# w2's low halves on VectorE, four w2 buffers, two steps moved to GpSimd, and a new planned order

## The chip, the core and the metric

The kernel runs on one core of a Trainium2 chip. The metric is the device time of one launch in microseconds, the median of several runs. The core has four compute engines that run side by side, each through its own queue in the order that the program fixes: TensorE (PE in the profile; matmuls and transposes, results in PSUM), VectorE (DVE), ScalarE (ACT) and GpSimd (POOL). A fifth queue, SyncE (SP), issues DMAs.

## The reference

Attention with a top-32 mask in float32, then two feed-forward blocks with float64 weights, each block's result rounded to float32; 2 x 576 tokens, 8 heads of 64.

```
scores = q @ k.T / 8                    # per head, 576 x 576
kth = 32nd largest of each row
scores = where(scores >= kth, scores, -1e9)
attn = exp(scores - max); attn = attn / (attn.sum(-1) + 1e-9)
x = concat_heads(attn @ v)              # 1152 x 512
h = x @ w_in                            # 2048 wide
x = (max(h, 0) + alpha * min(h, 0)) @ w_out
out = ((x @ w_a) * (x @ w_b)) @ w_out2  # 1536 wide
```

## The kernel before

**Work and groups.** The query rows are cut into six groups (M1, counted 0 to 5): two of 128 tokens from the first batch, three of 256 tokens, one of 128. Every group's attention consists of tiles of 128 query rows of one head, 72 in all. A tile's scores go through TensorE (`front`), then VectorE finds the 32 largest by four rounds of MAX8 and three of MATCH_REPLACE8 (`middle`, lines 1094 to 1103) and multiplies mask and exponentials with a running sum (line 1110, tiles e and sm). ScalarE adds 1e-9 to that sum (line 1111), VectorE takes the reciprocal (line 1117), and GpSimd scales e with it (line 1118). `back` transposes (on TensorE for batch 0, by a transposing DMA on SP for batch 1), and `av` multiplies with v, one pair of heads at a time, into xT.

**The two feed-forward blocks.** Each group runs `moe1` and `moe2` in the order of ORDER and STAGES. `moe1`'s `l1` makes h (tiles h, from wi), the leaky relu follows, and `l2` projects with wo into y; `moe2`'s `l3` makes hab (from wa and wb) and `l4` projects with w2 into o. The first groups run in float32 ("native") weights; from the third group on, and in the first layer of the second group, a product is made of three half-precision passes ("split"): high times high, high times low, low times high.

**The relu of a native second layer.** GTM gives the way for groups 0, 1, 2. For 'd' (lines 1306 to 1312) ScalarE writes both relus, the negative one back into PSUM, and VectorE blends them in one instruction. For 'p' (lines 1309, 1317, 1318) the negative one goes to SBUF, and GpSimd multiplies it by minus alpha and adds the other. 'm' alternates by block.

**Weights.** Each 128 x 512 block of a weight comes as float64 and is converted (`to_f32`) by ScalarE, VectorE and GpSimd together; w2's 12 float32 blocks are then parked in device memory (w2_st). After `scales` (the tot matmul at line 764 and its copy at 766) `pair` turns blocks into a high and a low half: ScalarE scales into the tile wsc (tag tmp, one buffer) and rounds it to the high half, GpSimd subtracts for the low half. For w2 (lines 893 to 902) a block is loaded from w2_st into a w2s tile, the halves are made in a second w2s tile, and that is stored to w2_pr, from which `moe2` loads (line 1386). The w2s tiles are W2B = 3 buffers, handed out in the order of the program.

**Order.** `tile_topk_attention_moe` emits three tracks (attention and conversion, pairs, feed-forward). `keep_planned_order` then replays all instructions in a model of the chip (`planned_order`: durations from NS, a due time of each instruction from its place plus RANK, buffers handed out in turn) and fixes for every engine the order that comes out of it.

Of the kernel before, what the change touches and what calls it, by code (L numbers as in the profile page):

```python
# [11 lines left out]
F32 = mybir.dt.float32  # L12
# [29 lines left out]
W2B = 3  # L42
# [15 lines left out]
PAIRS = ("wi", "wo", "wa", "wb", "w2")  # L58
# [7 lines left out]
GTM = 'mdd'  # L66
# [26 lines left out]
    "ACT Activation Copy S4x1024h<-S4x1024f": (1056, 947, None),  # L93
    "ACT Activation Copy S4x128f<-P4x128f": (277, 157, None),
    "ACT Activation Copy S4x128f<-P4x128f,S4x1f": (367, 265, None),
    "ACT Activation Copy S4x128h<-P4x128f": (277, 173, None),
    "ACT Activation Copy S4x128h<-P4x128f,S4x1f": (367, 250, 2465),
    "ACT Activation Copy S4x128h<-S4x128f": (309, 258, None),
    "ACT Activation Copy S4x1f<-S4x1f": (203, 93, 2095),
    "ACT Activation Copy S4x256f<-P4x256f,S4x1f": (469, 357, 2863),  # L100
    "ACT Activation Copy S4x256h<-P4x256f": (383, 281, None),
    "ACT Activation Copy S4x256h<-P4x256f,S4x1f": (473, 356, None),
    "ACT Activation Copy S4x256h<-S4x256f": (416, 307, 2428),
    "ACT Activation Copy S4x256r<-S4x256f": (417, 306, None),
    "ACT Activation Copy S4x512f<-P4x512f": (597, 477, None),
    "ACT Activation Copy S4x512f<-S4x512f,S4x1f": (721, 613, None),
    "ACT Activation Copy S4x512h<-P4x512f,S4x1f": (687, 570, None),
    "ACT Activation Copy S4x512h<-S4x512f": (619, 520, None),
    "ACT Activation Copy S4x513s<-S4x513u": (791, 639, None),
    "ACT Activation Copy S4x576f<-P4x576f": (647, 530, 2039),  # L110
    "ACT Activation Copy S4x576h<-S4x576f": (683, 589, 2124),
    "ACT Activation Copy S4x576r<-S4x576f": (682, 574, None),
    "ACT Activation Copy S4x640f<-S4x640f,S4x1f": (829, 721, None),
    "ACT Activation Copy S4x640h<-S4x640f": (730, 627, None),
    "ACT Activation Copy S4x64h<-P4x64f": (218, 104, None),
    "ACT Activation Copy S4x64h<-P4x64f,S4x1f": (305, 196, None),
    "ACT Activation Copy S4x64r<-S4x64f": (244, 146, None),
    "ACT Activation Exp P4x576f<-S4x576f,S4x1f": (745, 666, None),
    "ACT Activation Relu P4x128f<-P4x128f": (284, 195, None),
    "ACT Activation Relu P4x128f<-P4x128f,S4x1f": (367, 249, 2425),  # L120
    "ACT Activation Relu S4x128f<-P4x128f": (272, 150, None),
    "ACT Activation Relu S4x128f<-P4x128f,S4x1f": (382, 249, 2465),
    "ACT Activation Sign S4x513b<-S4x513f": (777, 626, None),
    "ACT Activation Square S4x512f/<-P4x512f": (680, 570, None),
    "ACT Activation Square S4x640b/<-S4x640f": (824, 719, None),
    "ACT DMACopy  D2x512f<-S2x512f": (542, 580, 2660),
    "ACT DMACopy  D4x512f<-S4x512f": (338, 394, 2017),
    "DVE MatchReplace  S4x576f<-S4x8f,S4x576f": (811, 733, None),
# [1529 lines left out]
```

## Time and profile before

| | |
|---|---|
| runs (three) | 677.06, 678.73, 679.77 us; median 678.73 |
| profiled execution | 680.37 us, of which the span of its instructions 678.6 |
| granted TensorE clock, mean | 0.956 |
| busy: TensorE | 610.2 us (90%) |
| busy: VectorE | 552.0 us (81%) |
| busy: ScalarE | 482.6 us (71%) |
| busy: GpSimd | 435.8 us (64%) |
| DMA | 94.84 MB, 140 GB/s over the span |

The shares are means over phases with different limits. In the table of windows a window's first figure is its length; a busy time near it means that the engine is full there. In an order of time, the bracket at the end of a row gives the idle time before the instruction and what ended it. A group's "idle before" is the idle time of its engine just ahead of it. TensorE's clock has two levels, and the granted clock is a window's mean in shares of the higher.

### The profile page before, as it was taken

Reading aid. Unit: us, or ns where it says so; the run is one execution under the profiler, and the core shown is the slowest. Engines: PE = TensorE matmul, PEld = TensorE weight load, DVE = VectorE, ACT = ScalarE, POOL = GpSimd, SP = SyncE. Lnnn points to the kernel's source line nnn. Section 1 sums busy time; section 2 is a strip of 40 time slices with the busy share of each in tenths; the row PEclk is TensorE's granted clock in tenths of the full one; section 3 lists DMA queues with packets and bytes.
Section 4 is the critical chain, followed back from the end, with each engine's and each line's share of the span. In section 5 each row is a group of like instructions: output and inputs, shape, how many; then the busy total and the mean of one; then the engine's idle time right before and its main releaser. Section 6 shows DMA issues by size and latency. Waiting matters only on the chain.

```text
span 678.6 us, 14869 instructions
## 1 busy us (share of the span) xinstructions
PE 610.2 (90%) x5094; PEld 448.4 (66%) x5094; DVE 552.0 (81%) x1340; ACT 482.6 (71%) x1051; POOL 435.8 (64%) x648
## 2 busy tenths in 40 slices
PE   2466689999999999599979799999999999999997
PEld 1355477787766877467648477665877776777775
DVE  4999999869999999989999899999999997320021
ACT  5799999997899988799888455565655564642232
POOL 5787689976766877888988555554666556222221
PEclk9976689999999999699999899999999999999999
DMA  6997899984421132223576854522345332002243
GB/s 182 331 321 247 269 366 337 355 297 137 118 89 50 45 105 64 82 78 100 149 182 160 177 128 97 123 44 51 86 104 117 86 81 42 12 2 63 63 141 109
DMA packets 98491, 94.84 MB, mean 140 GB/s; under 512 B 50416, under 2 KB 72688, under 8 KB 98416
## 3 DMA queue, kind: packets, MB, share of 16 engines
q1 hardware_dynamic: 97104, 91.54, 47.7%
q10 hardware_dynamic: 1312, 2.36, 1.0%
q8 instruction: 40, 0.66, 0.4%
q14 instruction: 35, 0.29, 0.1%
HBM read 74.60 MB, written 8.65 MB: 123 GB/s over the span
## 4 chain that ended last, share of the span: by engine, by line
PE 42%; DVE 4%; DMA 4%; ACT 2%; issue 1%; POOL 0%; POOLq 0%; SPq 0%; ACTq 0%; DVEq 0%
PE hab L1258 13%; PE h L1258 9%; PE o L1270 8%; PE y L1270 7%; DMA w2s<-w_st 2%; PE ps L1083 2%; PE o L1170 2%; DVE wk L1101 1%; DVE m L1103 1%; DMA pt<-e 1%; DVE e L1110 1%; DMA kr<-in_kT_dram 1%; DVE yb L1344 0%; ACT w2s L900 0%; ACT wsc L899 0%
## 5 line engine op out<-in xcount | busy, mean ns | idle before, releaser
L1103 DVE MAX8 m<-wk 128x8 f32<-128x576 f32 x216 | 162.9, 754 | 2.3
L1249 POOL TENSOR_TENSOR gp<-gt,gp 128x256 f16<-128x256 f32 (+1 forms) x112 | 68.1, 612 | 79.9 <-ACT gp L1248 79.4
L1101 DVE MATCH_REPLACE8 wk<-m,wk 128x576 f32<-128x576 f32 x144 | 107.0, 743 | 0.0
L1258 PE MATMUL h<-xT,wi_sb 128*128 128x256 f16 (+1 forms) x960 | 99.2, 251 | 0.9 <-DVE gt L1299 0.9
L1258 PEld LDWEIGHTS <-wi_sb 128*128 128x128 f16 x960 | 78.4, 98 | 23.4 <-issue 8.5
L1270 PEld LDWEIGHTS <-gp 128*128 128x128 f16 x588 | 54.7, 98 | 55.1 <-issue 4.7
L1270 PE MATMUL y<-wo_sb,gp 128*128 128x512 f16 x336 | 81.4, 379 | 0.9 <-ACT gp L1248 0.9
L1118 POOL TENSOR_SCALAR e<-e,sm 128x576 f32<-128x576 f32 x72 | 54.0, 749 | 35.6 <-DVE sm L1117 33.2
L1248 ACT ACTIVATE gp<-gt 128x256 f16<-128x256 f32 (+1 forms) x112 | 43.0, 388 | 39.8 <-PE y L1270 13.6
L1258 PE MATMUL hab<-xT,wa_sb 128*128 128x256 f16 (+1 forms) x648 | 67.0, 249 | 3.9 <-ACT xT L1349 3.7
L1083 PE MATMUL ps<-ks,qh 128*128 128x288 f32 x160 | 47.0, 377 | 23.1 <-DVE e L1110 14.0
L1270 PE MATMUL o<-w2s,gp 128*128 128x512 f16 x252 | 64.8, 388 | 1.8 <-DMA w2s<-w_pr 1.6
L1258 PE MATMUL hab<-xT,wb_sb 128*128 128x256 f16 (+1 forms) x648 | 64.2, 249 | 0.0
L1258 PEld LDWEIGHTS <-wa_sb 128*128 128x128 f16 x648 | 52.1, 98 | 16.5 <-issue 4.1
L1094 DVE MAX8 m<-s 128x8 f32<-128x576 f32 x72 | 53.9, 749 | 10.2 <-ACT s L1086 10.0
L1110 DVE SCALAR_TENSOR_TENSOR e<-s,m,ep 128x576 f32<-128x576 f32 x72 | 58.3, 810 | 4.7 <-PE t L1143 1.3
L1431 DVE SCALAR_TENSOR_TENSOR gt<-hab,wb_inv,r 128x256 f32<-128x256 f32 (+1 forms) x36 | 15.6, 433 | 55.2 <-ACT r L1425 55.1
L1258 PEld LDWEIGHTS <-wb_sb 128*128 128x128 f16 x648 | 52.3, 98 | 4.1
L1107 ACT ACTIVATE ep<-s,nb 128x576 f32<-128x576 f32 x72 | 53.8, 747 | 1.5 <-ACT s L1086 0.4
L842 ACT ACTIVATE rlo<-raw 128x513 int16<-128x513 uint32 x68 | 52.4, 788 | 2.3 <-DMA raw<-in_wo_dram 1.8
L1101 DVE MATCH_REPLACE8 wk<-m,s 128x576 f32<-128x576 f32 x72 | 53.5, 743 | 0.0
L1086 ACT ACTIVATE s<-ps 128x576 f32<-128x576 f32 x72 | 46.6, 647 | 9.5 <-PE ps L1083 9.2
(204 smaller groups left out, 1394.6 us busy)
## 6 DMA issues: line engine op xcount, KB each, us to landing
w2s<-w_pr SPq DMA_DIRECT2D x48, 256.0 KB, 2.7
w2s<-w_st SPq DMA_DIRECT2D x36, 256.0 KB, 3.1
raw<-in_wi_dram SPq DMA_DIRECT2D x16, 516.0 KB, 5.7
raw<-in_wo_dram SPq DMA_DIRECT2D x16, 516.0 KB, 5.5
raw<-in_wa_dram SPq DMA_DIRECT2D x12, 516.0 KB, 5.9
raw<-in_wb_dram SPq DMA_DIRECT2D x12, 516.0 KB, 5.6
raw<-in_w_dram SPq DMA_DIRECT2D x12, 516.0 KB, 5.1
kr<-in_kT_dram SPq DMA_DIRECT2D x32, 144.0 KB, 3.0
```

Source lines behind the costliest of these rows:

```text
L842: nc.scalar.activation(r.bitcast(I16).rearrange("p (a n t) -> p a n t", a=3, t=2)[:, :, :, 0], lo, AF.Copy, scale=2.0 ** -29)
L1083: nc.tensor.matmul(ps[:, f, 0:HALF], q[:, h % 2, :], ks[h][:, f * HALF:(f + 1) * HALF], start=i == 0, stop=i == len(mm) - 1)
L1086: nc.scalar.activation(s.rearrange("p (a n) -> p a n", a=2), ps[:, :, 0:HALF], AF.Copy)
L1094: nc.vector.max(m8[:, 0:8], s)
L1101: nc.vector.match_replace(out=wk, in_to_replace=m8[:, 8 * r - 8:8 * r], in_values=src, imm_value=NEG)
L1103: nc.vector.max(m8[:, 8 * r:8 * r + 8], wk)
L1107: nc.scalar.activation(ep, w2(s), AF.Exp, bias=nb, scale=0.125)
L1110: nc.vector.scalar_tensor_tensor(w2(e), w2(s), m8[:, 31:32], ep, op0=ALU.is_ge, op1=ALU.mult, accum_out=sm[:, 0:1])
L1118: nc.gpsimd.tensor_scalar(e, e, sm[:, 1:2], LIFT if tl["lift"] else 1.0, op0=ALU.mult, op1=ALU.mult)
L1249: nc.gpsimd.tensor_sub(l[:, 0:n], t[:, 0:n], h[:, 0:n])
L1258: nc.tensor.matmul(dst[:, 0:n], w[a][:, c * P:(c + 1) * P], x[:, b, c, 0:n], start=k == 0, stop=k == 11)
L1270: nc.tensor.matmul(dst, act[b][:, s], w[a], start=i == 0 and k == 0, stop=i == last and k == 2)
```

## The change

Five things change. `pair` hands w2 to a new `moved_pair`: ScalarE writes the scaled block straight into the high half, and VectorE makes the low half as block times scale minus high half, reading the unscaled block; the tmp tile, the second ScalarE pass and GpSimd's subtraction are gone for w2. There are four w2s buffers. The 1e-9 is added by GpSimd. The second group's native relu takes the way 'p' for all its 16 blocks. And the order is planned anew: the pairs of wa and wb are emitted in turn, the planner's durations and all its ranks have new values, TensorE keeps a tile shape longer (STAY), ScalarE and SP may wait a little for an instruction that is due earlier (LOOK, MARGIN), and the model lets no more than eight DMAs run at once.

```diff
-W2B = 3
+W2B = 4
-PAIRS = ("wi", "wo", "wa", "wb", "w2")
+MOVED = ("w2",)
+PAIRS = [(n, i) for n in ("wi", "wo") for i in range(8)] + [(n, i) for i in range(6) for n in ("wa", "wb")] + [("w2", i) for i in range(6)]
+CHAIN = [p for p in PAIRS if p[0] in MOVED and p[0] != "w2"]
+HOME = {p: q for p, q in zip(CHAIN, [None] + CHAIN)}
-GTM = 'mdd'
+GTM = 'mpd'
...
+STAY = 1235
+LOOK = {"PE": 0, "DVE": 0, "ACT": 100, "POOL": 0, "SP": 150}
+MARGIN = {"PE": 1090, "DVE": 4640, "ACT": 3550, "POOL": 3050, "SP": 3330}
...
-        k = heapq.heappop(ready[e])[1]
+            heapq.heappush(ready[e][ops[k].tile], (p, k))
+        stays = lambda p, of: p - (STAY if e == "PE" and of == tile else 0)
+        best = min(((stays(r[0][0], of), of) for of, r in ready[e].items() if r), default=None)
+        if c and c[0][0] <= t + LOOK[e] and stays(c[0][1], ops[c[0][2]].tile) + MARGIN[e] < best[0]:
+            t, _, k = heapq.heappop(c)
+        else:
+            k = heapq.heappop(ready[e][best[1]])[1]
         x = ops[k]
...
+        if x.moves:
+            t = max(t, lanes[moved % 8])
...
+    def moved_pair(name, i, common):
+        sc = wsc[name][:, 0:1] if common else wsc[name][:, i:i + 1]
+        for j in range(2):
+            f = 2 * i + j
+            if name == "w2":
+                w = w2_tile()
+                nc.sync.dma_start(w, w2_st[f])
+                v = w2_tile().bitcast(F16)
+            else:
+                w, v = wsb[name][:, f], home(name, i)[:, j].bitcast(F16)
+            s1 = wo_sig[:, f:f + 1] if name == "wo" else sc
+            nc.scalar.activation(v[:, 0:DM], w, AF.Copy, scale=s1)
+            nc.vector.scalar_tensor_tensor(v[:, DM:2 * DM], w, s1, v[:, 0:DM], op0=ALU.mult, op1=ALU.subtract)
+            if name == "w2":
+                nc.sync.dma_start(w2_pr[f], v)
+
     def pair(name, i, common):
+        if name in MOVED:
+            moved_pair(name, i, common)
+            return
...
-        nc.scalar.activation(sm[:, 1:2], sm[:, 0:1], AF.Copy, bias=1e-9)
+        nc.gpsimd.tensor_scalar(sm[:, 1:2], sm[:, 0:1], 1e-9, None, op0=ALU.add)
...
-        for name in PAIRS:
+        for name, i in PAIRS:
...
-            for i in range(NBLK[name] // 2):
-                fs = (2 * i, 2 * i + 1)
-                while name != "w2" and not all((name, f) in native_used for f in fs):
-                    yield None
...
+            pair(name, i, name in ("wo", "w2"))
+            for f in (2 * i, 2 * i + 1):
+                pair_done[name, f] = clock["bg"] + T_PAIR
+            yield T_PAIR
```

`home` and HOME give weights other than w2 a new place when they are in MOVED; with w2 alone there, they change nothing.

## Rows read from the trace of the kernel before

**Rows 1.** Table of windows: span, busy us of each engine (instructions), clock, DMA share, GB/s.

```profile
core 0: us, PE busy (x) PEld busy (x) DVE busy (x) ACT busy (x) POOL busy (x), PEclk, DMA share, GB/s
20.00:100.00 80.00, 55.39 (x348) 40.97 (x348) 77.82 (x200) 75.99 (x151) 62.13 (x72) 0.74 0.91 304
120.00:160.00 40.00, 37.65 (x310) 29.68 (x309) 31.63 (x90) 35.60 (x78) 32.87 (x38) 1.00 0.84 284
185.00:219.00 34.00, 33.56 (x274) 22.17 (x271) 33.41 (x83) 32.80 (x79) 22.17 (x27) 1.00 0.24 71
260.00:300.00 40.00, 32.06 (x209) 22.56 (x207) 35.56 (x77) 33.05 (x67) 32.10 (x59) 0.83 0.26 76
300.00:340.00 40.00, 39.15 (x338) 27.75 (x338) 38.39 (x91) 35.27 (x77) 36.42 (x60) 1.00 0.45 119
317.00:379.00 62.00, 55.09 (x572) 40.91 (x571) 58.24 (x141) 52.06 (x115) 54.30 (x83) 1.00 0.66 164
340.00:386.00 46.00, 37.81 (x424) 29.73 (x424) 41.58 (x101) 34.86 (x75) 34.66 (x52) 1.00 0.76 172
400.00:582.00 182.00, 179.85 (x1500) 127.68 (x1498) 170.77 (x393) 103.19 (x231) 102.53 (x164) 1.00 0.38 83
582.00:678.60 96.60, 92.56 (x967) 70.45 (x965) 17.36 (x48) 35.52 (x94) 24.23 (x46) 0.99 0.22 67
```

**Rows 2.** TensorE in order of time, 255 to 300 us: start, us, instruction, idle before.

```profile
272.20 0.71 PE L1258 MATMUL h<-xT,wi_sb 128*128 128x256 f16 x5
...
275.47 0.52 PE L1083 MATMUL ps<-ks,qh 128*128 128x288 f32 x2 [1.70 <-DVE e L1110]
...
293.18 0.38 PE L1258 MATMUL h<-xT,wi_sb 128*128 128x256 f16 x2
```

**Rows 3.** VectorE in order of time, 100 to 160 us.

```profile
141.96 0.17 DVE L766 COPY tot_s<-tot 128x8 f32<-128x8 f32 x1 [5.58 <-PE tot L764]
```

**Rows 4.** Chain of waits that ended last: start us, us, what.

```profile
337.25 4.08 DMA w2s<-w_st
...
379.50 6.21 DMA pt<-e
```

**Rows 5.** The tile w2s from 300 to 400 us: min/median/max ns, first and last start.

```profile
L1270 PE MATMUL o<-w2s,gp x36: 377/379/631, 379.0 to 398.1; 128*128 128x512 f16 x36
L899 ACT ACTIVATE wsc<-w2s,w_sc x12: 708/722/738, 317.5 to 375.1; 128x512 f32<-128x512 f32 x12
L900 ACT ACTIVATE w2s<-wsc x12: 613/621/643, 319.3 to 376.1; 128x512 f16<-128x512 f32 x12
L901 POOL TENSOR_TENSOR w2s<-wsc,w2s x12: 1157/1162/1173, 321.8 to 376.9; 128x512 f16<-128x512 f32 x12
```

**Rows 6.** Groups of instructions by line, over the span: busy us, mean ns | idle before, releaser.

```profile
L1118 POOL TENSOR_SCALAR e<-e,sm 128x576 f32<-128x576 f32 x72 | 54.0, 749 | 35.6 <-DVE sm L1117 33.2 <-DMA v<-in_vL_dram 0.8 <-POOL ks L981 0.4
...
L1095 POOL TENSOR_SCALAR nb<-m 128x1 f32<-128x1 f32 x72 | 15.4, 214 | 13.7 <-DVE m L1094 13.3
...
L1111 ACT ACTIVATE sm<-sm 128x1 f32<-128x1 f32 x72 | 14.5, 201 | 29.8 <-DVE e L1110 29.4
...
L1117 DVE RECIPROCAL sm<-sm 128x1 f32<-128x1 f32 x72 | 11.1, 154 | 2.9 <-ACT sm L1111 2.8
...
L1312 DVE SCALAR_TENSOR_TENSOR gp_n<-h,nalpha,r_n 128x128 f32<-128x128 f32 x24 | 8.0, 341 | 0.4 <-ACT h L1309 0.4
...
L1303 ACT ACTIVATE r_n<-h,pre_true 128x128 f32<-128x128 f32 x16 | 5.7, 367 | 0.6 <-PE h L1258 0.4
...
L1309 ACT ACTIVATE h<-h,pre_tneg 128x128 f32<-128x128 f32 x16 | 5.4, 345 | 0.0
...
L1344 DVE SCALAR_TENSOR_TENSOR yb<-y,ysq,yb 128x512 f16<-128x512 f32 x7 | 5.2, 741 | 1.0 <-ACT yb L1343 1.0
...
L1318 POOL TENSOR_TENSOR gp_n<-r_n 128x128 f32<-128x128 f32 x8 | 3.7, 465 | 0.0
...
L1317 POOL TENSOR_TENSOR r_n<-r_n,nalpha 128x128 f32<-128x128 f32 x8 | 3.2, 403 | 0.3 <-ACT r_n L1309 0.2
```

More of the change, by code (lines that the diff above doesn't have):

```diff
@@ new lines @@
+    "ACT Activati xT<-o": 491,
+    "ACT Activati xT<-o,vsc": 2236,
+    "ACT Activati xT<-tp": 3789,
+    "ACT Activati xe<-o": -843,
+    "ACT Activati xe<-tp": 730,
+    "ACT Activati yb<-y": -7110,
+    "ACT Activati yb<-y,ysq": -22801,
+    "ACT DMACopy out_0_dram<-ob": 16383,
+    "DVE MatchRep wk<-m,s": 8455,
+    "DVE MatchRep wk<-m,wk": 13843,
+    "DVE Max m<-s": 10388,
+    "DVE Max m<-wk": 7309,
+    "DVE Reciproc sm<-sm": -843,
+    "DVE TensorCo amax<-rmb": 6790,
+    "DVE TensorCo ident<-ident": 6790,
@@ new lines @@
+    "PE Matmult y<-wo_sb,gp": 28998,
+    "PE Matmult y<-wo_sb,gp_n": 12829,
+    "POOL Memset ident<-": -5270,
+    "POOL Memset ones<-": -5270,
+    "POOL Memset qh<-": -34788,
+    "POOL Memset ql<-": -14149,
+    "POOL Memset v<-": -653,
+    "POOL Memset v_raw<-": -4070,
+    "POOL Memset vp<-": -6257,
+    "POOL TensorSc e<-e,sm": -4532,
+    "POOL TensorSc ident<-ident": -5270,
+    "POOL TensorSc nalpha<-alpha": -5270,
+    "POOL TensorSc nb<-m": -5997,
+    "POOL TensorSc sm<-sm": -1939,
@@ L607, in planned_order @@
             gates[k] += 1
[L608 removed]
+    ready, coming, free = ({e: defaultdict(list) for e in HOP}, {e: [] for e in HOP}, {e: 0.0 for e in HOP})
     def arrive(k):
@@ L874, in halves, with home @@
     def halves(name, f):
-        v = (w2_tiles[f] if name == "w2" else wsb[name][:, f]).bitcast(F16)
+        v = w2_tiles[f] if name == "w2" else home(name, f // 2)[:, f % 2]
+        v = v.bitcast(F16)
         return v[:, 0:DM], v[:, DM:2 * DM]
+    spare = []
+    def home(name, i):
+        place = HOME.get((name, i), (name, i))
+        if place is None:
+            if not spare:
+                spare.append(late[0].tile([P, 2, DM], F32, tag="tmp", name="spare", bufs=TB))
+            return spare[0]
+        name, i = place
+        return wsb[name][:, 2 * i:2 * i + 2]
     def scales(name, common):
@@ L1566, in bg_track @@
                 yield 1.0
-            for i in range(NBLK[name] // 2):
-                fs = (2 * i, 2 * i + 1)
-                while name != "w2" and not all((name, f) in native_used for f in fs):
-                    yield None
-                clock["bg"] = max([clock["bg"]] + [native_used.get((name, f), 0) for f in fs])
-                pair(name, i, name in ("wo", "w2"))
-                for f in fs:
-                    pair_done[name, f] = clock["bg"] + T_PAIR
-                yield T_PAIR
+            place = HOME.get((name, i), (name, i))
+            fs = [(place[0], f) for f in (2 * place[1], 2 * place[1] + 1)] if place and name != "w2" else []
+            while not all(f in native_used for f in fs):
+                yield None
+            clock["bg"] = max([clock["bg"]] + [native_used[f] for f in fs])
+            pair(name, i, name in ("wo", "w2"))
+            for f in (2 * i, 2 * i + 1):
+                pair_done[name, f] = clock["bg"] + T_PAIR
+            yield T_PAIR
     def need_block(name, f, split):
```

507 lines of the change are left out of this document (238 added, 269 removed).

## The prediction

> **What bounds the kernel now.** I read the page's engine shares first (the table above): TensorE and VectorE are both nearly full over the span. That says nothing on where a microsecond can be won, so I read the table of windows next [rows 1]. The reader is to see three phases in it. From 20 to 100 us VectorE is full (77.8 of 80 us) and TensorE has only 55.4 us of work, at a granted clock of 0.74: the kernel is waiting for top-k and for the weights to be converted. From 400 to 582 us both are full (179.9 and 170.8 of 182). From 582 us TensorE runs alone for 96.6 us on the stages that need no more attention. So VectorE fixes when the last attention group is done, and TensorE's tail hangs behind it; but TensorE can only use an earlier date if it has less work left over, so time is won only where both lose idle time earlier on. TensorE's idle time that can be talked about lies from 260 to 386 us: 7.9 us in 260 to 300, 0.9 in 300 to 340, 8.2 in 340 to 386, together 17.0 us [rows 1].
>
> The order of time on TensorE shows the cause of the first hole [rows 2]. The wide h matmuls of the third group stop after 272.8 us, when 18 have been issued (three of four contraction steps of two blocks; the last five stand there), and come back at 293.2. In between the engine waits for VectorE's e, 1.70 us the first time, and the granted clock over the window is 0.83 [rows 1]: the fourth pair of heads had not come out of top-k. That hole is thus VectorE's, and whatever VectorE lost before 291 us is in it. It lost most of it from 120 to 160 us: busy 31.6 of 40, so 8.4 us idle, 5.58 of them in one wait for the totals of wi [rows 1, 3], while ScalarE stood at 35.6 of 40.
>
> The chain of waits shows the second hole [rows 4]: from 337 us it runs through loads of stored w2 blocks (4.08 us the one shown) and ends in a 6.21 us transposing DMA. The w2 tile shows why [rows 5]: ScalarE's scaling, its rounding and GpSimd's subtraction run over the 12 blocks from 317.5 to 376.9 us, one block in 5 us, and the first o matmul of the third group begins at 379.0. All 12 blocks go through three buffers and each holds two of them, and the scaled copy goes through a single tmp tile.
>
> **The change part by part.** The sum is made against the profiled execution: 680.37 us, its span 678.6 and 1.8 around it. The median of the runs is 678.73, 1.6 lower, so the result is lowered by 1.6 at the end.
>
> w2 halves. Removed: 12 roundings of 0.621 us on ScalarE (7.5 us), 12 subtractions of 1.162 us on GpSimd (13.9 us) [rows 5] and the tmp tile. ScalarE keeps one activation a block (0.72 us, now straight to half precision). Added: 12 fused multiply-subtracts on VectorE. Their nearest row is the same operation on 512 columns out of PSUM, 741 ns [rows 6]: 12 x 0.741 = 8.9 us. From 317 to 379 us VectorE is busy 58.2 of 62 [rows 1], so at most 3.8 us of that goes into holes and the rest pushes top-k back. Arithmetic of one block falls from 0.72 + 0.62 + 1.16 = 2.5 us to about 1.5, plus the wait for VectorE's queue (one top-k instruction is 0.75 us), and four buffers instead of three let one more load be under way. By itself I take that as 5 us off the second hole's 8.2, but it is worth only as much as VectorE can follow; it is not added again below.
>
> The second group's blend. 16 blocks lose one VectorE instruction of 341 ns: 16 x 0.341 = 5.5 us, all of it between 185 and 219 us, where VectorE is at 33.4 of 34 [rows 1, 6]. So the group that ends at 293 can come 5.5 us earlier. GpSimd gets 16 x (0.403 + 0.465) = 13.9 us [rows 6]. It is busy 22.2 of 34 there [rows 1], and with the additions below it would need 37 of 34: about 3 us of other GpSimd work (halves of wi and wo) has to move behind 219, or the projections wait. ScalarE's second relu goes to SBUF instead of PSUM: 0.345 us becomes that of the first, 0.367 [rows 6], +0.4 us in all, beside the rest.
>
> The 1e-9. ScalarE loses 72 x 0.201 = 14.5 us and 29.4 us of waiting for VectorE's e in its queue; GpSimd gets 72 x about 0.214 = 15.4 us (the row of its other one-column operation, nb) [rows 6], of which about 1 us lies between 185 and 219. The waiting goes along with it: behind it on GpSimd are queued the subtractions for gp, on which TensorE's projections hang. GpSimd's queue waits 33.2 us for the reciprocal one step later anyway, so I take this as nothing on the path; the bounds are minus 2.8 us (VectorE's waits for ScalarE's 1e-9) and plus 72 x 0.107 = 7.7 us, if each addition held up one gp for half its own length [rows 6].
>
> The order. wa and wb pairs alternate, the planner keeps TensorE longer on one tile shape and looks ahead on ScalarE and SP, and all priorities are new. The trace prices it only from both sides. What it could win is VectorE's idle time before 400 us: 8.4 (120 to 160), 4.4 (260 to 300), 1.6 (300 to 340) and 4.4 (340 to 386) [rows 1], together 18.8 us. What it could lose has no floor but that of a plan as bad as the 20 to 100 window. I take the single 5.6 us wait of the first window, since ScalarE is relieved just there, and half of the other 10.4: together 10.8 us.
>
> Sum on VectorE, which is the sum for the end: -5.5 (blend) + 8.9 (w2) - 10.8 (holes) = -7.4 us. TensorE has 17.0 us of idle time and some 5.4 us of slow clock (17% of 32.1 us in 260 to 300) to give, so it can follow. 680.4 - 7.4 = 673.0, less 1.6: **671.4 us**. With none of the holes won it is 682.2 by the median, with all of them 663.4, and with the ends of the 1e-9 660.6 to 689.9.
>
> One rule bears against the change. No row here has a large VectorE instruction with two inputs in SBUF; the new w2 instruction is one, so its 0.741 us may be short. From the rows: GpSimd is busy 54.3 of 62 us there with 83 instructions, 0.65 us each [rows 1]; if the new instruction had to let a running one finish, it would wait 0.88 x 0.33 = 0.29 us on average, 3.4 us over 12, at most 12 x 1.16 = 14. That is a rival below. The Trainium skill states this mechanism (SBUF — State Buffer, Who interferes with whom): a VectorE instruction with two SBUF inputs and a GpSimd instruction that reads SBUF lock each other out for a whole instruction. No run here shows it yet; by it the sum would be 674.8.
>
> **The rivals.** *The plan gets much more* (chance 0.18): VectorE's holes close and the clock stays up from 273 to 300. For it: both holes have one cause each and both causes are touched. Against it: VectorE's load is lower by 5.5 before 293 but higher by 8.9 after. -16 to -20 us: 659 to 663.
>
> *VectorE pays for w2 and nothing comes back* (0.22), the other side: VectorE is already at 58.2 of 62 where the 8.9 us go, the last group's top-k is later by 8.9 - 5.5 = 3.4, and the tail of 96.6 us with it; 682.2 without the 1e-9, 686 with half of its 7.7 us. It decides if VectorE's idle time before 400 us does not fall by at least 3.4 us. For it: in the middle stretches (33.4 of 34 us from 185 to 219) nothing is loose; against it: the 18.8 us of holes.
>
> *Lock-out on the port* (0.08): forecast plus 3.4, 674.8 (with its bound 685). *GpSimd becomes the bound of the second group* (0.06): the 3 us too much delay projections between 185 and 219, where TensorE is at 33.6 of 34; 674.5. *The pieces cancel* (0.08), the gain of the plan eaten by the new waits of GpSimd: 677 to 680.
>
> **How the numbers follow.** Forecast 671.4 (0.38), own range 666 to 675. A measurement of this kernel can tell about 0.5% from no change, 3.4 us: faster is below 675.3, slower above 682.1. Faster: 0.38 + 0.18 + half of port and GpSimd (0.07) = 0.63. Same: the other half (0.07), the cancelling (0.08) and a third of the VectorE rival (0.07) = 0.22. Slower: the rest of that rival, 0.15. The range 658 to 684 holds the forecast, the better plan, the cancelling and the lower half of the VectorE rival; what it leaves out is that rival's upper half and the ends of the bounds.
>
> **What would show each step.** In the changed profile: VectorE's busy time up by 3 to 4 us, ScalarE's down by some 22, GpSimd's up by some 15; the fused w2 instruction at 0.74 us (lock-out: well above or with gaps that end with GpSimd); the wide h matmuls of the third group resuming before 288 instead of 293; the last w2 half before 370 and the first o of the third group before 374; the tail after the last top-k as long as now, 100 us. The forecast is wrong if VectorE's idle time up to the last top-k is not smaller by about 10 us, or if it is smaller and TensorE still has a 15 us hole between 260 and 390.

## The result and the profile after

The changed kernel takes 681.84 us (median of nine runs), the kernel before, run beside it, 677.80: a ratio of 1.0054, with a 95% interval of 1.0039 to 1.0070. It is 4 us slower, where 7.3 us faster was forecast. The profiled execution took 683.72 us, its span 681.9, against 680.37 and 678.6.

The table of windows of the changed kernel, over the stretches of [rows 1]:

```profile
core 0: us, PE busy (x) PEld busy (x) DVE busy (x) ACT busy (x) POOL busy (x), PEclk, DMA share, GB/s
20.00:100.00 80.00, 48.63 (x335) 36.45 (x336) 73.90 (x190) 70.38 (x135) 60.67 (x80) 0.79 0.91 300
120.00:160.00 40.00, 36.72 (x306) 28.92 (x304) 38.71 (x104) 38.89 (x78) 35.82 (x44) 1.00 0.92 311
185.00:219.00 34.00, 34.00 (x308) 24.18 (x309) 31.95 (x75) 30.48 (x67) 29.57 (x58) 1.00 0.30 86
260.00:300.00 40.00, 33.94 (x225) 25.11 (x224) 39.02 (x80) 31.93 (x65) 30.80 (x64) 0.87 0.46 139
300.00:340.00 40.00, 36.87 (x328) 26.36 (x327) 37.01 (x80) 34.53 (x70) 33.58 (x55) 1.00 0.59 162
340.00:386.00 46.00, 43.35 (x430) 31.58 (x429) 44.07 (x107) 33.77 (x64) 38.01 (x63) 0.96 0.49 98
```

Read the VectorE column against [rows 1]. The hole from 120 to 160 us is closed (31.63 busy became 38.71), the one from 260 to 300 too (35.56, now 39.02). But from 20 to 100 us VectorE has lost 3.9 us (77.82, now 73.90) and TensorE is busy 6.8 us less (55.39, now 48.63, with 13 fewer instructions and a granted clock of 0.79 instead of 0.74), and from 300 to 340 us VectorE has lost 1.4 (38.39, now 37.01). The window from 160 to 260 us, a row of each kernel, before and then after, shows 3.7 us lost again:

```profile
160.00:260.00 100.00, 97.52 (x734) 72.61 (x733) 97.84 (x247) 92.07 (x202) 71.16 (x104) 1.00 0.31 90
```

```profile
160.00:260.00 100.00, 96.00 (x715) 72.23 (x714) 94.16 (x237) 85.78 (x181) 80.53 (x143) 0.98 0.31 91
```

The third group and w2 in the changed kernel: TensorE in order of time (start us, us), as in [rows 2], and the tile w2s, as in [rows 5]:

```profile
274.33 2.13 PE L1302 MATMUL h<-xT,wi_sb 128*128 128x256 f16 x18
...
292.11 0.38 PE L1302 MATMUL h<-xT,wi_sb 128*128 128x256 f16 x2 [1.52 <-ACT xT L1227]
```

```profile
L1314 PE MATMUL o<-w2s,gp x36: 379/379/390, 370.6 to 397.1; 128*128 128x512 f16 x36
L926 ACT ACTIVATE w2s<-w2s,w_sc x12: 707/713/723, 277.4 to 332.5; 128x512 f16<-128x512 f32 x12
L927 DVE SCALAR_TENSOR_TENSOR w2s<-w2s,w_sc x12: 731/867/1548, 278.8 to 333.7; 128x512 f16<-128x512 f32 x12
```

The low halves of w2 are now made from 278.8 to 333.7 us, 43 us ahead of before, and the first o matmul comes at 370.6 instead of 379.0. The wide h matmuls come back at 292.11 instead of 293.18. The groups that answer to [rows 6] (columns as there):

```profile
L1162 POOL TENSOR_SCALAR e<-e,sm 128x576 f32<-128x576 f32 x72 | 53.9, 749 | 22.1 <-DVE sm L1161 18.7 <-DVE ysq L772 1.4 <-PE o L1317 0.7
L1155 POOL TENSOR_SCALAR sm<-sm 128x1 f32<-128x1 f32 x72 | 15.7, 218 | 29.3 <-DVE e L1154 23.5 <-DVE e L771 1.7
L927 DVE SCALAR_TENSOR_TENSOR w2s<-w2s,w_sc 128x512 f16<-128x512 f32 x12 | 12.1, 1010 | 0.4 <-ACT w2s L926 0.4
L1161 DVE RECIPROCAL sm<-sm 128x1 f32<-128x1 f32 x72 | 11.0, 153 | 2.8 <-POOL sm L1155 2.4
L1362 POOL TENSOR_TENSOR gp_n<-r_n 128x128 f32<-128x128 f32 x24 | 10.8, 461 | 0.2
L1361 POOL TENSOR_TENSOR r_n<-r_n,nalpha 128x128 f32<-128x128 f32 x24 | 9.4, 403 | 0.6 <-ACT r_n L1353 0.6
```

GpSimd's queue now waits 23.5 us for VectorE's e ahead of the 1e-9, and VectorE waits 2.4 us for the 1e-9, about as long as it waited for ScalarE's. The one price that is off is that of VectorE's w2 instruction: 1,010 ns, not 741.

**Where the 3.3 us come from.** The profiled executions differ by 3.3 us, the medians by 4.0. The last of the 72 reciprocals starts at 571.5 us before and at 574.8 after (the tile sm, min/median/max ns, first and last start; after):

```profile
L1155 POOL TENSOR_SCALAR sm<-sm x72: 207/213/534, 20.4 to 574.6; 128x1 f32<-128x1 f32 x72
L1161 DVE RECIPROCAL sm<-sm x72: 132/153/164, 20.7 to 574.8; 128x1 f32<-128x1 f32 x72
```

From there to the end both take 107.1 us. So the whole of it lies ahead of the last top-k, on VectorE, where the account up to the last e is: w2 +12.1, the blend -5.5, idle time -5.1 (39.2 became 34.1, the time that no VectorE instruction covers), and +1.8 because neighbouring instructions overlap less (70.4 us of overlap in VectorE's records up to there before, 68.6 after; the instructions apart from w2 and the blend take no longer than before): together +3.3. Two dates say where. The 32nd and the 40th e, before and then after (in order of time on VectorE):

```profile
281.23 0.81 DVE L1110 SCALAR_TENSOR_TENSOR e<-s,m,ep 128x576 f32<-128x576 f32 x1
...
341.51 0.81 DVE L1110 SCALAR_TENSOR_TENSOR e<-s,m,ep 128x576 f32<-128x576 f32 x1
```

```profile
277.34 0.80 DVE L1154 SCALAR_TENSOR_TENSOR e<-s,m,ep 128x576 f32<-128x576 f32 x1
...
346.64 0.82 DVE L1154 SCALAR_TENSOR_TENSOR e<-s,m,ep 128x576 f32<-128x576 f32 x1 [0.19 <-ACT r L1342]
```

At the 32nd the changed kernel is 3.9 us ahead, at the 40th 5.1 us behind. The 9 us that lie between these two figures are lost in the stretch in which VectorE does w2.

### The profile page after: what moved, and what is told of

It is laid out like the page before. It is cut to its first block, busy times and chain, and to the rows that moved or that the text cites. A ratio compares the mean times of both kernels' runs of the same rounds, so it can differ in the third digit from the quotient of the medians.

```text
span 681.9 us, 14845 instructions
## 1 busy us (share of the span) xinstructions
PE 605.9 (89%) x5094; PEld 448.1 (66%) x5094; DVE 560.3 (82%) x1336; ACT 468.4 (69%) x967; POOL 452.3 (66%) x740
## 4 chain that ended last, share of the span: by engine, by line
PE 36%; DVE 9%; POOL 4%; DMA 4%; ACT 3%; issue 2%; SPq 1%; POOLq 0%; ACTq 0%; DVEq 0%
PE hab L1302 13%; PE o L1314 7%; PE h L1302 7%; PE y L1314 5%; DVE wk L1145 3%; DVE m L1147 3%; DMA pt<-e 2%; PE o L1214 2%; PE ps L1127 2%; DVE e L1154 1%; DVE gt L1343 1%; POOL gp L1293 1%; POOL e L1167 1%; DVE m L1138 1%; DMA kr<-in_kT_dram 1%
## 5 line engine op out<-in xcount | busy, mean ns | idle before, releaser
L1293 POOL TENSOR_TENSOR gp<-gt,gp 128x256 f16<-128x256 f32 (+1 forms) x112 | 67.9, 610 | 88.4 <-ACT gp L1292 87.4
L1469 ACT ACTIVATE r<-hab,pre_wa 128x256 f32<-128x256 f32 (+1 forms) x48 | 21.4, 445 | 62.0 <-PE hab L1302 58.3
L1314 PE MATMUL o<-w2s,gp 128*128 128x512 f16 x252 | 63.2, 380 | 0.1
L1302 PEld LDWEIGHTS <-wa_sb 128*128 128x128 f16 x648 | 52.8, 99 | 14.6 <-issue 2.1
```

The costliest lines, as they stand in the source:

```text
L1293: nc.gpsimd.tensor_sub(l[:, 0:n], t[:, 0:n], h[:, 0:n])
L1302: nc.tensor.matmul(dst[:, 0:n], w[a][:, c * P:(c + 1) * P], x[:, b, c, 0:n], start=k == 0, stop=k == 11)
L1314: nc.tensor.matmul(dst, act[b][:, s], w[a], start=i == 0 and k == 0, stop=i == last and k == 2)
```

## The experiments

**The theories.** Theory 1: VectorE's bill, what the pieces add to its work is what is lost. Theory 2: the pieces are cheap and the new order is the loss. Theory 3: GpSimd's queue is the loss, since the 1e-9 and the blend stand in it ahead of others. Theory 4 was formed after the first twelve runs: each order is fitted to its own pieces, and an order that isn't fitted costs more than any piece.

In the kernels a_... (but for a_ctrl and a_jit) every engine runs the changed kernel's order, written down, with one thing exchanged, in b_... (but for the two b_jit) the order of before with one thing put in. A new instruction stands at the planned time of the one that it replaces; in b_w2dve and b_blend_pool it stands right behind the ScalarE instruction that it needs. All medians and ratios are against the kernel before on the same chip (677.3 to 678.3 us). The last two columns are the start of the last reciprocal and the rest of the span behind it, in the profiled execution. That of before took 680.37 us, some 2 to 3 us above its medians, and that of the changed kernel 683.72, 1.9 above: a single date is that uncertain, so the verdicts go by the medians and ratios.

| kernel | median us | ratio [95%] | last reciprocal | rest |
|---|---|---|---|---|
| before | 677.3 to 678.3 | 1 | 571.5 | 107.1 |
| after | 681.84 | 1.0054 [1.0039, 1.0070] | 574.8 | 107.1 |
| a_ctrl | 681.61 | 1.0068 [1.0044, 1.0092] | 572.4 | 107.1 |
| a_w2pool | 687.64 | 1.0155 [1.0131, 1.0179] | 578.3 | 107.1 |
| a_sm_act | 683.97 | 1.0095 [1.0075, 1.0115] | 574.6 | 107.7 |
| a_blend_dve | 684.56 | 1.0111 [1.0088, 1.0135] | 574.0 | 107.0 |
| a_no_low | 679.61 | 1.0027 [1.0006, 1.0048] | 571.2 | 107.1 |
| a_one_input | 679.73 | 1.0033 [1.0014, 1.0052] | 569.7 | 107.2 |
| a_no_add | 682.77 | 1.0069 [1.0052, 1.0086] | 573.7 | 107.7 |
| b_w2dve | 686.18 | 1.0128 [1.0107, 1.0149] | 577.8 | 107.1 |
| b_blend_pool | 686.62 | 1.0127 [1.0107, 1.0147] | 577.1 | 107.1 |
| b_sm_pool | 687.97 | 1.0141 [1.0122, 1.0160] | 579.8 | 107.1 |
| b_all | 698.09 | 1.0292 [1.0270, 1.0313] | 589.2 | 107.1 |
| b_buf4 | 677.49 | 0.9992 [0.9979, 1.0005] | 569.6 | 107.1 |
| b_no_add | 677.79 | 1.0000 [0.9987, 1.0013] | 568.5 | 107.3 |
| x_bcode_aplan | 700.61 | 1.0335 [1.0291, 1.0378] | 575.9 | 123.8 |
| x_acode_bplan | 695.14 | 1.0255 [1.0220, 1.0289] | 574.0 | 120.4 |
| b_jit_small | 703.47 | 1.0392 [1.0351, 1.0434] | 581.5 | 125.2 |
| b_jit | 701.68 | 1.0359 [1.0337, 1.0382] | 577.9 | 121.7 |
| a_jit | 707.92 | 1.0448 [1.0426, 1.0469] | 582.5 | 122.0 |

### One piece undone in the new order

a_ctrl is the changed kernel itself, line for line, run beside the others.

> The changed kernel itself, so that the others of this call have it on the same chip. All theories: 680 to 683.

681.61 us against 681.84. Its profiled execution has the last reciprocal at 572.4 and not 574.8, w2 at 11.4 us instead of 12.1 and idle time of 32.8 us instead of 34.1, so the terms of the account above carry scatter of about 1 us and a date some 2 us. That writing an order down costs nothing by itself is seen in b_buf4 and b_no_add, which run the order of before, written down, in the time of before; in the traces of a_no_low and a_no_add all instructions that are left stand on every engine in the changed kernel's order.

a_w2pool gives w2's low halves back to GpSimd:

```diff
-nc.scalar.activation(v[:, 0:DM], w, AF.Copy, scale=s1)
-nc.vector.scalar_tensor_tensor(v[:, DM:2 * DM], w, s1, v[:, 0:DM], op0=ALU.mult, op1=ALU.subtract)
+nc.scalar.activation(w, w, AF.Copy, scale=s1)
+nc.scalar.activation(v[:, 0:DM], w, AF.Copy)
+nc.gpsimd.tensor_sub(v[:, DM:2 * DM], w, v[:, 0:DM])
```

> The changed kernel with the order of every engine kept as it is, and only w2's halves made as before: ScalarE scales the block in place and rounds it, GpSimd subtracts at the place where VectorE did; VectorE's 12 instructions are gone. Theory 1, VectorE's bill (the end is the last top-k plus a tail of 107.6 us, so each us on VectorE counts): VectorE loses 12.1 us between 278 and 334, the last top-k comes 6 to 12 us earlier, the time falls to 672 to 676. Theory 2, the new order itself is the loss and the pieces are neutral in it: 680 to 683. Theory 3, GpSimd's queue is the loss: with 14 us more on it the time rises, 683 to 690.

687.64 us, 6 slower than the changed kernel, although VectorE has 12 us less to do. Its idle time up to the last e rises from 34.1 to 47.2 us: its waits for GpSimd from 2.4 to 9.0, those for ScalarE's relu and scores (r and s) from 5.8 to 11.7. The time is in the range that theory 3 gave; theories 1 and 2 miss. ScalarE has its second pass back as well, so the run doesn't part the two engines.

a_sm_act gives the 1e-9 back to ScalarE, a_blend_dve the blend of the second group to VectorE (one instruction of 469 ns, both inputs in SBUF, for GpSimd's two; in the kernel before it was 341 ns out of PSUM, so this isn't the old form):

```diff
-nc.gpsimd.tensor_scalar(sm[:, 1:2], sm[:, 0:1], 1e-9, None, op0=ALU.add)
+nc.scalar.activation(sm[:, 1:2], sm[:, 0:1], AF.Copy, bias=1e-9)
...
-                if direct:
+                if direct or g == 1:
```

> The changed kernel, order kept, and only the 1e-9 back on ScalarE at the place in time that it had on GpSimd. Theory 1: VectorE's work is the same, 681 to 683. Theory 2: the same, 681 to 683. Theory 3, GpSimd's queue: 15.4 us and its 23.5 us of waiting for VectorE are off it, 674 to 679.

> The changed kernel, order kept, and only the second group's blend back on VectorE as one instruction a block (both inputs now in SBUF), in place of GpSimd's two. Theory 1: VectorE has 16 x 0.34 = 5.4 us more before the third group, plus what the port costs, so 685 to 690. Theory 2: no change, 680 to 683. Theory 3: GpSimd loses 13.9 us between 185 and 225, 675 to 680.

683.97 and 684.56 us, ratios 0.3% and 0.4% above that of a_ctrl (both intervals still touch its own). None of the three pieces can be taken back with a gain, so the loss is not one bad piece in an otherwise good order. Theory 3 falls for the 1e-9 and the blend, whose return was to give 2 to 8 us; for w2 it held.

### VectorE's w2 work, left out or made shorter

a_no_low leaves the 12 instructions out (the high halves are stored twice), a_one_input makes them a scaling without the subtraction:

```diff
-nc.vector.scalar_tensor_tensor(v[:, DM:2 * DM], w, s1, v[:, 0:DM], op0=ALU.mult, op1=ALU.subtract)
+nc.vector.tensor_scalar(v[:, DM:2 * DM], w, s1, None, op0=ALU.mult)
```

> The changed kernel, order kept, without VectorE's 12 w2 instructions: the low halves are left out, and the store writes the high half in both places, so the product with w2 is not the reference's. Theory 1 (the end is the last top-k plus 107.6 us): 12.1 us less on VectorE between 278 and 334, the last top-k 8 to 12 us earlier and the time 670 to 674. Theory 2, the order is the loss and VectorE's work is covered: 679 to 682. If TensorE takes over as the bound on the way: the tail longer than 107.6 and 674 to 678.

> The changed kernel, order kept, with VectorE's w2 instruction reading one SBUF input (block times scale; the subtraction of the high half is left out, so the result is not the reference's). If GpSimd's reads locked the two-input form out (1010 ns mean instead of 741), the instruction now takes 0.74 us or less each time, VectorE gains 3 to 5 us, 677 to 680. If the 1010 ns have another cause, they stay, and 680 to 683.

Both give 2 us back (679.61 and 679.73 against 681.61; their intervals just touch that of a_ctrl), and neither reaches before. a_no_low is where theory 2 had it; a_one_input lies in the range of a lock that falls away, but its instruction took 0.85 us on average and not 0.74 or less each time, so that it escapes the lock was wrong (the last section). Why so little comes back is seen in the table of windows of a_no_low:

```profile
260.00:300.00 40.00, 34.55 (x227) 25.45 (x225) 35.46 (x75) 32.50 (x65) 31.38 (x64) 0.87 0.50 146
300.00:340.00 40.00, 38.24 (x334) 27.06 (x334) 32.43 (x77) 35.28 (x71) 32.28 (x57) 1.00 0.58 168
```

VectorE is busy 67.9 us of the 80 instead of 76.0: of the 12.1 us left out, 8.1 stand in these two windows as idle time. Its longest waits from 260 to 345 us (line, released by, us in total, times, longest) are for ScalarE, 2.6 us and none in the changed kernel:

```profile
DVE gt L1357 <- ACT r L1356: 4.7, 3, 2.2
DVE m L1152 <- ACT s L1144: 3.0, 3, 1.7
```

So VectorE's bill is real where it is paid (the 9 us between the 32nd and the 40th e), but in a kept order only 2 us of it can be had back: the next engine stands right behind. Theory 1 alone falls.

**The lock-out.** The 12 instructions of the changed kernel in order of time, four of them, and some of GpSimd's instructions beside them:

```profile
278.80 1.27 DVE L927 SCALAR_TENSOR_TENSOR w2s<-w2s,w_sc 128x512 f16<-128x512 f32 x1
283.69 0.74 DVE L927 SCALAR_TENSOR_TENSOR w2s<-w2s,w_sc 128x512 f16<-128x512 f32 x1
287.46 1.49 DVE L927 SCALAR_TENSOR_TENSOR w2s<-w2s,w_sc 128x512 f16<-128x512 f32 x1
...
311.97 0.73 DVE L927 SCALAR_TENSOR_TENSOR w2s<-w2s,w_sc 128x512 f16<-128x512 f32 x1
```

```profile
278.35 1.17 POOL L957 TENSOR_TENSOR wb_sb<-wsc,wb_sb 128x512 f16<-128x512 f32 x1
...
282.99 0.22 POOL L1139 TENSOR_SCALAR nb<-m 128x1 f32<-128x1 f32 x1
285.71 1.16 POOL L957 TENSOR_TENSOR wa_sb<-wsc,wa_sb 128x512 f16<-128x512 f32 x1 [2.50 <-ACT wa_sb L955]
...
287.24 1.16 POOL L957 TENSOR_TENSOR wa_sb<-wsc,wa_sb 128x512 f16<-128x512 f32 x1
```

At 283.69 and 311.97 GpSimd does nothing, and the instruction takes 0.74 and 0.73 us. At 278.80 a GpSimd subtraction has 0.72 us to go, and it takes 1.27; at 287.46 there are 0.94 to go, and it takes 1.49. Each time it ends 0.55 us after GpSimd's. Over the 12 that makes 12.1 us instead of 12 x 0.731 = 8.8, 3.3 more. The Trainium skill (SBUF — State Buffer, Who interferes with whom) states this lock between a VectorE instruction with two SBUF inputs and a GpSimd instruction that reads SBUF; the trace agrees.

### One piece put into the old order

```diff
-nc.scalar.activation(t[:, j], w, AF.Copy, scale=sc)
-nc.scalar.activation(v[:, 0:DM], t[:, j], AF.Copy)
-nc.gpsimd.tensor_sub(v[:, DM:2 * DM], t[:, j], v[:, 0:DM])
+nc.scalar.activation(v[:, 0:DM], w, AF.Copy, scale=sc)
+nc.vector.scalar_tensor_tensor(v[:, DM:2 * DM], w, sc, v[:, 0:DM], op0=ALU.mult, op1=ALU.subtract)
```

is b_w2dve. The others are these lines, one each for b_blend_pool, b_sm_pool and b_buf4; b_all is all four:

```diff
-GTM = 'mdd'
+GTM = 'mpd'
...
-nc.scalar.activation(sm[:, 1:2], sm[:, 0:1], AF.Copy, bias=1e-9)
+nc.gpsimd.tensor_scalar(sm[:, 1:2], sm[:, 0:1], 1e-9, None, op0=ALU.add)
...
-W2B = 3
+W2B = 4
```

> The kernel before with its own order and its three w2 buffers, and only w2's low halves on VectorE, put in behind ScalarE's scaling; ScalarE's rounding and GpSimd's subtraction are gone. Theory 1: VectorE has 9 to 12 us more between 317 and 379, where it has 3.8 us of idle time, so 684 to 690. Theory 2: the piece is neutral, 677 to 679. Theory 3: GpSimd has 14 us less, 670 to 676.

> The kernel before with its own order, and only the second group's blend on GpSimd (two instructions a block, put in right behind ScalarE's second relu). Theory 1, VectorE's bill: 5.4 us less on VectorE before the third group, 672 to 676. Theory 3, GpSimd's queue: it is asked for 36 of 34 us between 185 and 219, projections and top-k wait for it, 679 to 684.

> The kernel before with its own order, and only the 1e-9 on GpSimd, at the place in time that it had on ScalarE. Theory 1: VectorE's work is the same, 675 to 679. Theory 3: GpSimd's queue now waits for VectorE's e 72 times with the projections' halves behind it, 680 to 686.

> The whole change except the new order: the order of the kernel before, with w2's low halves on VectorE, four w2 buffers, the 1e-9 and the second group's blend on GpSimd. If the pieces make the whole loss and the new order is neutral: 681 to 683, as the changed kernel. If the pieces cost more and the new order gives part back: 684 to 692. If the new order is the loss: 674 to 679.

> The kernel before, its engine orders kept, with a fourth w2 buffer and nothing else. Theory 1 (VectorE sets the end, and w2's loads wait for buffers beside it): no change, within 2 us of 678. Rival (the 4.08 us waits for stored w2 blocks were what held the second hole): 3 to 6 us faster, 672 to 675.

The three pieces cost 8.9, 8.6 and 10.0 us when put in one by one, and 20.1 when all are in; the fourth buffer does nothing (0.9992, interval across 1), as theory 1 had it against the rival. w2 is where theory 1 had it; the two steps on GpSimd go the way of theory 3, each 2 to 3 us beyond its range, and b_all is 6 us beyond the highest range given. The rest behind the last reciprocal stays at 107.1 us in all of them, so each pays on VectorE's way to the last top-k.

For the 1e-9, the tile sm of b_sm_pool (idle time of the waiting engine, us, times):

```profile
L1132 DVE RECIPROCAL sm<-sm x72: 131/155/166, 20.7 to 579.8; 128x1 f32<-128x1 f32 x72
...
  DVE e L1125: 24.0, 23
  DVE sm L1132: 13.9, 27
  POOL sm L1126: 11.5, 23
```

VectorE waits 11.5 us for GpSimd's 1e-9 where it waited 2.8 for ScalarE's [rows 6], 8.7 more, and its last reciprocal is 8.3 later. That GpSimd's queue reaches the small step late, behind what was planned ahead of it, is the likely reason; no run tests it.

For the blend, the window from 185 to 219 us of b_blend_pool, and VectorE and ScalarE in order of time there:

```profile
185.00:219.00 34.00, 30.81 (x261) 20.26 (x258) 27.19 (x58) 28.59 (x67) 29.50 (x52) 1.00 0.21 64
```

```profile
199.17 1.15 ACT L932 ACTIVATE wsc<-wi_sb,wi_sc 128x1024 f32<-128x1024 f32 x1 [0.95 <-POOL wi_sb L935]
...
204.03 0.16 DVE L1139 RECIPROCAL sm<-sm 128x1 f32<-128x1 f32 x1 [2.11 <-ACT sm L1133]
...
206.39 1.33 ACT L930 ACTIVATE wsc<-wo_sb,wo_sig 128x512 f32<-128x512 f32 x2 [0.60 <-POOL wi_sb L935]
```

The 5.5 us are gone from VectorE, but it stands idle for 6.8 of the 34 us, 0.6 before. 4.3 of the 6.8 are four waits for ScalarE's 1e-9, of which before has none in this window. The rows fit this chain: GpSimd, at 29.50 us instead of 22.17, gives the one tmp tile back later; ScalarE waits for that with its scaling; ScalarE's 1e-9 stands behind it, and VectorE waits for that. This is the rival of GpSimd in the second group, in the old order, though by another way than the projections that it named. In the new order the same window has TensorE at 34.00 of 34 and VectorE at 31.95.

### Planner and pieces exchanged, and ranks moved

x_bcode_aplan is the changed kernel with the four pieces undone and the new planner and ranks kept (instructions that only the kernel before has keep its ranks and durations); x_acode_bplan is the kernel before with the four pieces put in and its own planner and ranks. Both are planned anew. For x_bcode_aplan:

```diff
-MOVED = ("w2",)
+MOVED = ()
...
-W2B = 4
+W2B = 3
...
-GTM = 'mpd'
+GTM = 'mdd'
...
-nc.gpsimd.tensor_scalar(sm[:, 1:2], sm[:, 0:1], 1e-9, None, op0=ALU.add)
+nc.scalar.activation(sm[:, 1:2], sm[:, 0:1], AF.Copy, bias=1e-9)
```

x_acode_bplan has the edits of b_all.

> The pieces of the kernel before (w2's low halves on GpSimd, three buffers, 1e-9 on ScalarE, blend on VectorE) planned by the new planner with its new ranks and the alternating pairs. Theory 1: VectorE's work is that of before and only the holes differ, 674 to 679. Theory 2, the new planner's order is the loss: 681 to 690. Theory 3, GpSimd's queue: 675 to 679.

> The changed pieces with four buffers, planned by the planner of before with its ranks (the ranks of the three new instructions are those of the changed kernel). The pieces of before under the new planner took 700.6, so ranks fitted to other pieces cost much. If that is general: 690 to 705. If it is the new planner that is bad by itself and the old one is sound: 678 to 686.

1.0335 and 1.0255: 700.61 us is 10 us beyond every range given for x_bcode_aplan, 695.14 lies in the one for ranks fitted to other pieces. As they stand, the new planner is no gain for the old pieces, and the old one is none for the new. Where it is lost is seen in the last column of the table: in x_acode_bplan VectorE is through at 574.0 us, as in the changed kernel, but 120.4 us remain instead of 107.1. TensorE has more work left at that date.

That could be the pieces or the fit, so the next three change no piece at all. Each rank is moved by a random amount, up to 0.2 us (b_jit_small, two of its lines) or 1 us (b_jit, a_jit):

```diff
-    "DVE TensorSc e<-s,m,ep": 432,
+    "DVE TensorSc e<-s,m,ep": 602,
...
-    "POOL TensorSc e<-e,sm": -2854,
+    "POOL TensorSc e<-e,sm": -2808,
```

> The kernel before with every rank of its planner moved by a random amount of up to 0.2 us and the order planned anew; nothing else is changed. Theory 4 (each old order is fitted to its own pieces, and any other order of the same quality of planner costs about as much as the new one gave back): 5 to 12 us slower than before, 683 to 690. Rival (the planner finds an order of the same worth from any ranks near these, so that the exchange of planners lost its 20 us by the pieces and not by a lost fit): within 3 us of before.

> The same with random amounts of up to 1 us. Theory 4: 12 to 25 us slower than before, in the place of the two exchanges of planner and pieces (694 to 701). Rival: within 5 us of before.

> The changed kernel with every rank of its planner moved by a random amount of up to 1 us and planned anew. Theory 4: 10 to 25 us slower than the changed kernel, 692 to 707. Rival (the new planner with its wider choice is robust): within 5 us of the changed kernel, 680 to 687.

All three lose 23 to 26 us: 703.47 and 701.68 against 678.27, and 707.92 against 681.84. The smaller movement costs as much as the larger one, twice what theory 4 expected of it; of the other two, b_jit is at the upper end of what it expected and a_jit 1 us beyond. Its rivals, which saw no more than 5 us, fall. Each is a single random draw. TensorE from the last e on, in b_jit and in before:

```profile
577.00:699.60 122.60, 117.52 (x1157) 84.85 (x1154) 23.25 (x66) 44.37 (x117) 32.38 (x58) 0.99 0.20 56
```

```profile
571.00:678.60 107.60, 103.56 (x1063) 76.77 (x1061) 20.27 (x59) 39.95 (x105) 28.35 (x52) 0.99 0.22 63
```

TensorE has 117.52 us of work left instead of 103.56, and it is busy 96% of the time in both. Of b_jit's 21 us of span, 6.4 lie ahead of the last reciprocal and 14.6 in this backlog. So the two exchanges (17 and 23 us) lost no more than moved ranks cost, and say nothing for or against the new planner; theory 2 can't be decided by them.

### The 1e-9 left out

The running sum holds the largest element's own exponential, about 1, so that 1e-9 doesn't change the float32. The step can go:

```diff
-nc.scalar.activation(sm[:, 1:2], sm[:, 0:1], AF.Copy, bias=1e-9)
...
-nc.vector.reciprocal(sm[:, 1:2], sm[:, 1:2])
+nc.vector.reciprocal(sm[:, 1:2], sm[:, 0:1])
```

> The kernel before, its engine orders kept, with the 1e-9 step left out: the reciprocal reads the running sum itself. The sum holds the largest element's own exponential, about 1, and 1e-9 is below half a unit in the last place of such a float32, so the output stays what it was. It gives the price of the 1e-9 wherever it stands. Theory 1 (only VectorE's own waits count): before waits 2.8 us for ScalarE's step, so 2 to 4 us faster, 674 to 676. Theory 3 (the queue that holds the step is what costs: 14.5 us of work and 29.4 us of waiting leave ScalarE): 5 to 9 us faster, 669 to 673.

> The changed kernel, its engine orders kept, with the 1e-9 step left out in the same way. Theory 1: VectorE waits 2.4 us for GpSimd's step there, so 2 to 3 us faster than the changed kernel, 678 to 680. Theory 3: GpSimd loses 15 us of work and 23.5 us of waiting, and the projections behind it come earlier: 5 to 9 us faster, 672 to 677.

Nothing in either order: 1.0000 [0.9987, 1.0013] against before, and 682.77 us against 681.84 for the changed kernel. In b_no_add the 72 steps (14.5 us on ScalarE) and their 29.4 us of waiting in its queue are gone, and VectorE's wait of 2.8 us with them; its wait for ScalarE's scores rises from 10.0 to 11.6. All four expectations fell: a step of 72 instructions, for which VectorE waits 23 times if it is put elsewhere, is worth nothing where the order was planned around it.

No kernel here beats before beyond what can be measured; b_buf4 and b_no_add are level with it.

## Why the prediction was wrong

The sum was -7.4 us on VectorE and came out at +3.3, 10.7 off. The ending was as forecast: the rest behind the last top-k is the same as before, and what VectorE loses ahead of it is what the kernel loses.

- **The holes** are the step that failed, 5.7 of the 10.7 us. 10.8 us were to come from VectorE's idle time, 5.1 did. The gain itself came: the wait for the totals of wi [rows 3] is gone, the 120 to 160 window gave 7.1 us where 5.6 were taken, and the three other windows gave 4.6 where 5.2 were taken, together 11.7. What failed is that the sum put the new order's losses at nothing: outside these four windows VectorE lost 6.5 us, 3.9 from 20 to 100 and 3.7 from 160 to 260 with small gains beside them. In the second, it waits 2.9 us for ScalarE's scores, before for none. In the first, it waits 4.1 us for loads of wo, before 1.4. Two of these loads are issued at 16.62 and 21.29 us, before at 15.20 and 19.10; VectorE stands before its conversions, the first of them before, and two after:

```profile
20.40 0.69 DVE L844 TENSOR_SCALAR wo_sb<-raw 128x513 int32<-128x513 int32 x1 [0.35 <-DMA raw<-in_wo_dram]
```

```profile
23.91 0.69 DVE L857 TENSOR_SCALAR wo_sb<-raw 128x513 int32<-128x513 int32 x1 [2.37 <-DMA raw<-in_wo_dram]
...
30.30 0.69 DVE L857 TENSOR_SCALAR wo_sb<-raw 128x513 int32<-128x513 int32 x1 [1.76 <-DMA raw<-in_wo_dram]
```

  The first conversion is 3.5 us later, its load was issued 1.4 later: the order on SP is a part of it, and a longer way from issue to landing the rest. No run tests what made it longer. The text gave the order a loss that "has no floor" and then put it into the sum with gains alone, although 20 to 100 was the window it named as the worst.
- **w2 on VectorE** was mis-sized: 12.1 us, not 8.9. The whole 3.2 is the lock-out, which stood as a rival at 3.4 and is shown above; in a_ctrl, the same kernel, it makes 2.6. Its place moved too: the work lies from 278.8 to 333.7 us and not from 317 to 379. The last 1.8 of the 10.7 is the smaller overlap of VectorE's instructions, which the sum put at nothing.
- **The blend** gave the 5.5 us on VectorE, and the 32nd e came 3.9 us earlier. Put into the old order it costs 8.6 us, since GpSimd is overfull, as the rival said, but over the tmp tile, ScalarE and VectorE and not over the projections.
- **The 1e-9** as nothing was right for the new order: VectorE waits 2.4 us for it, 2.8 before, and leaving it out changes nothing. The reason given, that GpSimd waits for the reciprocal anyway, was wrong: in the old order it costs 10.0 us, beyond the bound of 7.7, and not by gp but by VectorE's reciprocal, which the text named only as a gain.
- **The four buffers** were credited with part of the second hole. Alone they leave the time as it was. Nor does w2 on VectorE close it, which the text credited with 5 us: from 340 to 386 us, where TensorE had 8.2 us of idle time [rows 1], b_w2dve has 9.1 (b_all, with all four pieces, 9.5), and a_w2pool, with the halves on GpSimd but in the new order, 2.9 (b_w2dve, then a_w2pool):

```profile
340.00:386.00 46.00, 36.91 (x395) 28.43 (x393) 44.96 (x100) 30.17 (x63) 26.07 (x42) 0.93 0.58 147
```

```profile
340.00:386.00 46.00, 43.15 (x414) 31.12 (x414) 43.81 (x107) 33.49 (x63) 40.55 (x65) 0.96 0.48 104
```

  So it is the order, with its earlier place for w2, that closed the hole, and closing it made the kernel no faster.
- **What would show each step.** GpSimd's busy time rose by 16.5 us (15 forecast) and the first o came at 370.6 (before 374 forecast). ScalarE's busy time fell by 14.2, not 22: its groups lost 14.5 and 7.5, but some of that had run overlapped with others. VectorE's rose by 8.3 instead of 3 to 4. The wide h came back at 292.1, not before 288. Idle time up to the last top-k fell by 5.1, not 10, the sign named for a wrong forecast. TensorE's holes from 260 to 386 fell from 17.0 to 11.8 us.
- **The rival nearest to what came** is that VectorE pays for w2: it gave 682.2 us, and 681.84 was measured. Its own sign wasn't met: it was to decide if the idle time fell by less than 3.4, and it fell by 5.1. In the account the lock-out (3.3) and the smaller overlap (1.8) use that up, so the near number is in part luck. The account says where the time lies and not what taking a term out would give: with all 12 instructions left out, a_no_low got 2 us.

What stays open is what the pieces are worth with an order fitted as well as the old one. The old order with all pieces is 20.1 us slower than before, and the new order is 16 better than that; but moved ranks alone cost 23 us or more in each of the three draws, so neither figure is the price of the pieces or of the planner. Only a search of equal length for both would tell. So it stays open whether the 4 us are the pieces' or the order's. Not tried either is a load order on SP like the old one in the changed kernel.

## What to carry to other kernels

In a kernel whose engines run a planned order, the order itself carries much of the time (moved ranks alone: 23 us and more). Work that leaves an engine gives back little (12.1 us of VectorE left out: 2 us; 72 steps left out: nothing), and work that enters an engine with idle time isn't free (15.5 us of small steps on GpSimd, which was 64% busy: 10 us, most of it as a wait of VectorE). So price a move by the wait that it puts ahead of the bounding engine, and price "planned anew" by moving the ranks at random, not by the holes in the trace; an order that closes holes in one place can open others elsewhere, as from 20 to 100 and from 160 to 260 us here. And before giving VectorE an instruction with two SBUF inputs, count which GpSimd instructions will run beside it.

## What the runs showed of the hardware

The lock-out has a plain size: an instruction of VectorE that is locked out ends 0.55 us after GpSimd's, and all twelve agree with that or with their own 0.73 us within 0.02 (0.72 to go: 1.27; 0.94: 1.49; 1.00: 1.55). It holds in the other direction too: the 1e-9 on GpSimd that starts beside the first of them, at 279.60 us, took 0.53 us instead of 0.21 (the maximum in the tile sm above). GpSimd's memsets lengthened none of the twelve. Which engine is locked out goes by who starts first, and that can change from one execution to the next: the third of the twelve took 1.49 us above; in a_ctrl, the same kernel, it starts 0.07 us ahead of the subtraction, takes 0.73, and the subtraction 1.68 instead of 1.16:

```profile
285.22 0.73 DVE L927 SCALAR_TENSOR_TENSOR w2s<-w2s,w_sc 128x512 f16<-128x512 f32 x1
285.29 1.68 POOL L957 TENSOR_TENSOR wa_sb<-wsc,wa_sb 128x512 f16<-128x512 f32 x1
```

A scaling with one input is not free of it. The tile w2s of a_one_input:

```profile
L942 DVE TENSOR_SCALAR w2s<-w2s,w_sc x12: 468/842/1790, 275.4 to 328.4; 128x512 f16<-128x512 f32 x12
```

With GpSimd idle beside it, it takes 475 and 479 ns, two thirds of the fused one, but up to 1,790 beside GpSimd, on average 851, and here memsets lock it out too. The longest one starts with a subtraction of GpSimd and ends 0.28 us after the last of four memsets that follow that subtraction. The Trainium skill (SBUF — State Buffer, Who interferes with whom) counts this operation among those that can take the whole shared pair, and lets a two-input instruction contend only with GpSimd's reads: both agree with the memsets here.
